# Stage 2 of a three-part network on one Trainium2 core: projections, value tiles, output columns and softmax products at other score units

## The chip, the cores and the metric

The kernel runs on one core of a Trainium2 chip. The metric is the time of one execution on the device in microseconds (us). Five engines with instruction streams of their own work side by side: TensorE (PE, matmuls; PEld its weight loads), VectorE (DVE), ScalarE (ACT), GpSimd (POOL) and SyncE (SP), which issues the DMAs of this kernel. Each runs its instructions in the order in which they stand, and waits on semaphores for the others.

## The reference

Three layers follow each other for a batch of 8, sequence 576, width 512: attention with pooled keys and values, a gated MLP, and a mixture of four causal attention heads ("experts") with the two best of four taken by a gate. The change lies in the last layer:

```python
def _moe2_ref(x, w_gate, wq, wk, wv, wo):
    logits = x @ w_gate                      # top 2 of 4: weights w
    for e in range(E):                       # E = 4, head width 64
        q = x @ wq[e]; k = x @ wk[e]; v = x @ wv[e]
        scores = scale * (q @ k.transpose(0, 2, 1))
        scores = np.where(causal, -1e9, scores)
        scores = scores - scores.max(-1, keepdims=True)
        a = np.exp(scores)
        a /= a.sum(-1, keepdims=True) + 1e-9
        ye = a @ v @ wo[e]
        for kk in range(K):                  # K = 2
            mask = topk[:, :, kk] == e
            out += mask[..., None] * w[:, :, kk:kk + 1] * ye
    return out
```

## The kernel before

Stage 1 (class `PhaseA`) computes the first two layers for all 8 batches and leaves each batch's result in DRAM (`x2`), split into a high and a low part, since products of float32 are made here from three products of such parts. Stage 2 (class `PhaseB`) computes the last layer, batch by batch. Its output is transposed: columns of the result stand on partitions.

Stage 2 takes the four experts in two pairs p. Each batch has 2 x 9 **score units** (p, u): a block of 128 query rows of one expert, u = 1 to 4 of the first expert of the pair, 5 to 8 of the second, and u = 0 the last 64 rows of both. For a unit:

- `score` (L1036 to L1065): two or six matmuls into PSUM (L1047 to L1049, L1059 and L1060), mask and row minimum on VectorE (L1052, L1054, L1061), the exponential on ScalarE (L1064);
- `scale` (L1067 to L1081): the sum's reciprocal on VectorE (L1073, L1075, L1076), then the **softmax product** with that and the gate's weight (L1080), on VectorE for the units that the sets `SDF` (first batch) and `SDL` (last batch) name, on GpSimd for all others;
- `trans` (L1082 on), three units later (`LAG`): transposes on TensorE (L1093, L1106), copied out in a high part by ScalarE and a low part by VectorE (L1097, L1102, L1110, L1111);
- `av`, after the fifth and the last unit of a pair: the products with the values (L1126), two groups of columns.

Between the units stand the other steps, each as a word in a table. `10` to `13` are this batch's projections of pair 1 and `00` to `03` the next batch's of pair 0: q in two halves of the sequence, then k in two halves, twelve matmuls each (L931 to L933), copied out by ScalarE and VectorE. The last k half is followed by four DMAs that put k into the tile `kd` (L971), the last q half by two (L957). `v0` to `v4` are the next batch's **value tiles**, twelve matmuls (L1001 to L1003): three for each of the four chunks kc of its input x, in the order of kc; the gate's logits come with them, and `g` is the gate. `o0` to `o3` are the previous batch's **output columns**, four groups of three matmuls and more (L1148 to L1150), copied out by ScalarE, then stored. `x0` to `x3` load the next batch's four input chunks (L857, 576 KB each) into five slots that are used in turn, and GpSimd copies the last 64 columns of each into a tile for `v4` (L858). With five slots, `x0` finds one that is long free; `x1`, `x2` and `x3` take those that this batch's chunks 0, 1 and 2 leave, whose last reader is `13`.

The table `FILL` has for each p and u the words that follow the unit's scores and the scaling of the unit before; `FIRSTF` is for the first batch, `LASTF` for the last, and `PRE` has the steps ahead of the first unit. `run` goes through the units and writes the steps in this order; a scheduler then sets each engine's order from it, by its own estimates of when data come. It can hold a step's matmuls apart. PSUM has eight banks, each step takes the next that is free. SP's DMAs stand in one queue in the scheduler's order.

Of the kernel before, what the change touches and what calls it, by code (L numbers as in the profile page):

```python
# [822 lines left out]
LAG = 3  # L823
ALV = 1
KDM = 1
FILL = (('', '12 10 11', 'x0', '13 x1 x2 x3', '', '', 'o3 o1 o0', '', ''), ('v0', 'v1 00 02', '01 o2', '03', '', '', '', 'v2 v3', 'v4 g'))
FIRSTF = (('x0 10', '11', '12', '13 x1 x2 x3', '', '', '', '', ''), ('v0 00', '', '01 02 v1', '03', '', '', '', 'v2 v3', 'v4 g'))
LASTF = (('', '10 12 11', '', '', '13', '', 'o1', '', 'o0'), ('', '', '', '', '', 'o2', '', '', 'o3'))
SDF = {(0, 0), (0, 1), (0, 5), (0, 8), (1, 0), (1, 2), (1, 7)}
SDL = {(0, 4), (0, 6), (1, 6), (1, 7)}  # L830
PRE = 'v0 00 01 02 03 v1 v2 v3 v4 g'
AVS = [(0, 256), (256, S)]
LETTER = {mybir.EngineType.PE: "P", mybir.EngineType.Activation: "A", mybir.EngineType.DVE: "V", mybir.EngineType.Pool: "G",
          mybir.EngineType.SP: "S"}
# [5 lines left out]
class PhaseB:  # L840
# [226 lines left out]
    def scale(self, b, p, u):  # L1067
# [6 lines left out]
        else:  # L1074
# [3 lines left out]
        n = min(S, 128 * i + 128)  # L1078
        (nc.vector if (p, u) in (SDF if b == 0 else SDL if b + 1 == B else ()) else
         nc.gpsimd).tensor_scalar(pt[:, :n], pt[:, :n], st[:, 3:4], g, op0=OP.mult, op1=OP.mult)  # L1080
# [86 lines left out]
    def run(self):  # L1167
# [7 lines left out]
        def item(b, x):  # L1175
            if x[0] == "x":
                return [lambda: self.load_x(b + 1, int(x[1]))] if b + 1 < B else []
            if x[0] == "h":
                return [lambda: self.outp_head(int(x[1]))]
            if x[0] == "o":  # L1180
                return [lambda: self.outp(b - 1, int(x[1]))] if b > 0 else []
            if x == "1x":
                return [lambda: self.proj(b, "k", 1, 1, [lambda i=i: self.load_x(b + 1, i) for i in range(4 if b + 1 < B else 0)])]
            if x[0] == "1":
                return [part(b, 1)[int(x[1])]]
            if b + 1 == B:
                return []
            if x[0] == "0":
                return [part(b + 1, 0)[int(x[1])]]
            if x[0] == "v":  # L1190
                return [vpart(b + 1)[int(x[1])]]
            return [lambda: self.gate(b + 1)]
        for x in PRE.split():
            for f in item(0 if x[0] == "1" else -1, x):
                self.step("F", "p" + x, f)
        for k in range(len(units) + LAG + 1):
# [4 lines left out]
            if k < len(units):  # L1201
                b, p, u = units[k]
                for x in (LASTF if b + 1 == B else FILL if b else FIRSTF)[p][u].split():
                    for f in item(b, x):
# [76 lines left out]
```

## Time and profile before

| | us |
|---|---|
| median of 3 runs | 930.12 (929.57 to 930.19) |
| the profiled execution | 929.96 |
| its span, first to last instruction | 928.2 |
| TensorE busy in the span | 912.1 (98%) |
| VectorE busy | 674.5 (73%) |
| ScalarE busy | 515.4 (56%) |
| GpSimd busy | 407.2 (44%) |

The span is what the trace covers; the execution's own time is 1.76 us longer. Stage 2's first matmul starts at 555.24, after that each middle batch takes about 44.8 us. A matmul's busy time overlaps that of the next, so what one adds to TensorE is the distance from its start to the next start, and a wait shows as a start that comes late. The granted clock is 1.00 in all of stage 2 but the last microseconds.

### The profile page before, as it was taken

How to read it: one execution, taken by the hardware profiler on the slowest of the kernel's cores; microseconds unless marked ns; L12 is line 12 of the kernel's file. 1: busy time of each engine (PE TensorE's matmuls, PEld its weight loads, DVE VectorE, ACT ScalarE, POOL GpSimd, SP SyncE). 2: the span in 40 equal slices, each digit the busy share in tenths (PEclk: the TensorE clock that was granted, in tenths of full speed). 3: DMA queues.
4: the chain of work that ended last, by engine and by line, in shares of the span. 5: the costliest groups of instructions: out<-in, count | busy, mean ns of one | idle time of the engine just before them, and what ended most of it. 6: DMA issues, size and time to landing. Idle time of an engine off the chain costs nothing.

```text
span 928.2 us, 18390 instructions
## 1 busy us (share of the span) xinstructions
PE 912.1 (98%) x6518; PEld 858.2 (92%) x6518; DVE 674.5 (73%) x1851; ACT 515.4 (56%) x1273; POOL 407.2 (44%) x604
## 2 busy tenths in 40 slices
PE   8999999999999999999999999999999999999997
PEld 8579899899899899999998999899999999999987
DVE  7989587576676686675775436897878787878785
ACT  5775342443433434334433535677878677777786
POOL 1241576584693693693774440132323232323221
PEclk9999999999999999999999999999999999999999
DMA  9813323124124024033015124434434352514122
GB/s 324 297 57 121 130 74 124 65 85 150 39 74 164 25 74 177 12 111 140 22 43 204 32 90 134 127 115 114 126 104 141 88 154 76 177 52 152 52 63 78
DMA packets 42428, 101.81 MB, mean 110 GB/s; under 512 B 5472, under 2 KB 11616, under 8 KB 41440
## 3 DMA queue, kind: packets, MB, share of 16 engines
q1 hardware_dynamic: 42192, 100.63, 33.6%
q8 instruction: 52, 0.85, 0.4%
q14 instruction: 40, 0.33, 0.1%
q10 hardware_dynamic: 144, 0.00, 0.0%
HBM read 58.67 MB, written 28.31 MB: 94 GB/s over the span
## 4 chain that ended last, share of the span: by engine, by line
PE 80%; DVE 10%; ACT 4%; DMA 3%; issue 2%; SPq 1%; POOL 0%; ACTq 0%; DVEq 0%
PE op L643 4%; PE sc L362 4%; PE sp L615 4%; PE sp L617 4%; PE sp L616 4%; PE op L644 4%; PE op L645 4%; PE av L1126 3%; PE up L599 3%; PE up L601 3%; PE up L600 3%; PE vp L530 3%; PE vp L528 3%; PE vp L529 3%; PE t L1106 2%; PE tr L423 2%
## 5 line engine op out<-in xcount | busy, mean ns | idle before, releaser
L1080 POOL TENSOR_SCALAR pr<-pr,sm,gw 128x128 f32<-128x128 f32 (+3 forms) x119 | 72.1, 608 | 193.5 <-DVE sm L1076 129.8
L1064 ACT ACTIVATE pr<-s,sm 128x256 f32<-128x256 f32 (+4 forms) x160 | 83.1, 521 | 45.6 <-DVE sm L1061 20.7
L615 PE MATMUL sp<-wsh,vnh 128*128 128x288 f32 x256 | 78.0, 305 | 0.0
L643 PE MATMUL op<-g,woh 128*128 128x288 f32 x256 | 76.7, 305 | 0.3 <-DVE x2l L650 0.3
L644 PE MATMUL op<-g,woh 128*128 128x288 f32 x256 | 76.0, 297 | 0.0
L617 PE MATMUL sp<-wsl,vnh 128*128 128x288 f32 x256 | 75.5, 295 | 0.0
L616 PE MATMUL sp<-wsh,vnl 128*128 128x288 f32 x256 | 75.4, 295 | 0.0
L645 PE MATMUL op<-g,wol 128*128 128x288 f32 x256 | 74.3, 295 | 0.0
L599 PE MATMUL up<-x,wih 128*128 128x288 f32 x224 | 67.2, 300 | 0.0
L601 PE MATMUL up<-x,wil 128*128 128x288 f32 x224 | 66.2, 295 | 0.0
L600 PE MATMUL up<-x,wih 128*128 128x288 f32 x224 | 65.7, 293 | 0.0
L1061 DVE CUSTOM_DVE_ANT_0 s<-s,mk 128x512 f32<-128x512 f32 (+3 forms) x128 | 62.3, 487 | 3.0 <-PE t L1106 2.5
L1111 DVE TENSOR_TENSOR pbl<-t,pbh 128x512 fp32r<-128x512 f32 (+3 forms) x128 | 60.4, 484 | 2.3 <-ACT pbh L1110 1.0
L933 PE MATMUL pj<-xb,wql 128*128 128x288 f32 x208 | 61.4, 295 | 0.0
L931 PE MATMUL pj<-xb,wqh 128*128 128x288 f32 x208 | 61.3, 295 | 0.0
L932 PE MATMUL pj<-xb,wqh 128*128 128x288 f32 x208 | 61.2, 294 | 0.0
L1126 PE MATMUL av<-pbh,vt 128*128 128x320 f32 (+4 forms) x224 | 56.0, 279 | 2.7 <-ACT pbh L1110 2.7
L1106 PE MATMUL t<-ident,pr 128*128 128x128 f32 x320 | 56.2, 277 | 2.1 <-POOL pr L1080 2.1
L424 ACT ACTIVATE pth<-tr 128x640 fp32r<-128x640 f32 (+3 forms) x40 | 26.0, 652 | 52.0 <-PE tr L423 42.2
L580 ACT ACTIVATE vnh<-vg,rs 128x512 fp32r<-128x512 f32 (+1 forms) x40 | 27.2, 717 | 47.0 <-POOL rs L562 36.7
L1110 ACT ACTIVATE pbh<-t 128x512 fp32r<-128x512 f32 (+3 forms) x128 | 51.7, 441 | 2.4 <-PE t L1106 1.6
L558 DVE BATCH_NORM_STATS2 bs<-vg 128x6 f32<-128x512 f32 (+1 forms) x40 | 25.9, 681 | 35.6 <-ACT vg L531 35.1
(286 smaller groups left out, 3322.0 us busy)
## 6 DMA issues: line engine op xcount, KB each, us to landing
xb<-x SPq DMA_DIRECT2D x26, 576.0 KB, 5.3
kraw<-k_in SPq DMA_DIRECT2D x16, 576.0 KB, 3.9
x<-x2h SPq DMA_DIRECT2D x32, 288.0 KB, 2.1
x<-x2l SPq DMA_DIRECT2D x32, 288.0 KB, 2.1
kd<-scr SPq DMA_DIRECT2D x64, 144.0 KB, 2.5
out<-o SPq DMA_DIRECT2D x32, 288.0 KB, 2.8
vraw<-v_in SPq DMA_DIRECT2D x16, 512.0 KB, 4.3
pq<-q_in SPq DMA_DIRECT2D x7, 1152.0 KB, 6.9
```

The source lines that it names most:

```text
L599: nc.tensor.matmul(o, self.wi[0][:, kc, c], xh, start=kc == 0, stop=False)
L600: nc.tensor.matmul(o, self.wi[0][:, kc, c], xl, start=False, stop=False)
L601: self.upmm = nc.tensor.matmul(o, self.wi[1][:, kc, c], xh, start=False, stop=kc == 3).ins
L615: nc.tensor.matmul(o, vh[:, k, c], self.ws[0][:, k, s], start=k == 0, stop=False)
L616: nc.tensor.matmul(o, vl[:, k, c], self.ws[0][:, k, s], start=False, stop=False)
L617: nc.tensor.matmul(o, vh[:, k, c], self.ws[1][:, k, s], start=False, stop=False)
L643: nc.tensor.matmul(o, self.wo[0][:, k, c], gh[:, s], start=k == 0, stop=False)
L644: nc.tensor.matmul(o, self.wo[0][:, k, c], gl[:, s], start=False, stop=False)
L645: self.opmm = nc.tensor.matmul(o, self.wo[1][:, k, c], gh[:, s], start=False, stop=k == 3).ins
L1064: nc.scalar.activation(pt[:, s], o, AF.Exp, bias=st[:, 0:1], scale=-1.0, accum_out=st[:, 1 + 4 * j:2 + 4 * j])
L1106: nc.tensor.transpose(ps[:, j], pt[:, 128 * j:128 * j + 128], self.ident)
L1126: nc.tensor.matmul(ps[:, s - lo:], vt[:, j, 2 * p + e].rearrange("p a d -> p (a d)"), t[:, e, j * PTS + s:j * PTS + up], start=j == 0 and ...
```

## The change

The tables say other places. No instruction is added or taken away; five softmax products of the first batch leave VectorE and three come, three of the last batch come.

```diff
-FILL = (('', '12 10 11', 'x0', '13 x1 x2 x3', '', '', 'o3 o1 o0', '', ''), ('v0', 'v1 00 02', '01 o2', '03', '', '', '', 'v2 v3', 'v4 g'))
-FIRSTF = (('x0 10', '11', '12', '13 x1 x2 x3', '', '', '', '', ''), ('v0 00', '', '01 02 v1', '03', '', '', '', 'v2 v3', 'v4 g'))
-LASTF = (('', '10 12 11', '', '', '13', '', 'o1', '', 'o0'), ('', '', '', '', '', 'o2', '', '', 'o3'))
-SDF = {(0, 0), (0, 1), (0, 5), (0, 8), (1, 0), (1, 2), (1, 7)}
-SDL = {(0, 4), (0, 6), (1, 6), (1, 7)}
-PRE = 'v0 00 01 02 03 v1 v2 v3 v4 g'
+FILL = (('x0', '12 10 11', '', '13 x1 x2 x3', '', 'v0', 'o1 o0', 'o3 v1', ''), ('o2 00', '', '01', '02 03', '', '', 'v2', 'v3', 'v4 g'))
+FIRSTF = (('10', '11', 'x0 12', '13 x1 x2 x3', '', '', '', '', ''), ('00 01', 'v0', 'v1', '02 03', '', '', '', 'v2 v3', 'v4 g'))
+LASTF = (('', '10 12 11', '', '', '13', 'o1', '', '', ''), ('', '', '', 'o0', '', 'o2', '', '', 'o3'))
+SDF = {(0, 1), (0, 7), (0, 8), (1, 3), (0, 6)}
+SDL = {(0, 7), (1, 7), (0, 4), (1, 0), (1, 6), (1, 1), (0, 6)}
+PRE = '02 03 v0 v1 00 v2 01 v3 v4 g'
```

What the scheduler makes of it shows best at three places. In the rows below, names are tiles with their numbers: `s` and `s4` scores, `t` transposes, `vp` a value tile, `op` an output column, `xb` and `x4` the input chunks.

TensorE in batch 3, before: the scores of unit (0,5), the transposes of (0,2), the scores of (0,6), and the first matmuls of output column 3:

```order
L1059 MATMUL s_8234<-kd_5859,qs0_5803 128x512
L1060 MATMUL s_8234<-qs0_5803,qzvlo0_5812 128x512
L1106 MATMUL t_8242<-ident_90,pr_5819 128x128 x3
L1059 MATMUL s_8249<-kd_5859,qs0_5803 128x384
L1060 MATMUL s_8249<-qs0_5803,qzvlo0_5812 128x384
L1148 MATMUL op_8258<-ah_7847,wqh_5783 128x256
```

The same place now:

```order
L1059 MATMUL s_8234<-kd_5859,qs0_5803 128x512
L1060 MATMUL s_8234<-qs0_5803,qzvlo0_5812 128x512
L1001 MATMUL vp_8242<-wqh_5783,xb_5782 128x260
L1002 MATMUL vp_8242<-wqh_5783,xb_5782 128x260
L1003 MATMUL vp_8242<-wql_5784,xb_5782 128x260
L1001 MATMUL vp_8242<-wqh_5783,xb_5782 128x260
L1002 MATMUL vp_8242<-wqh_5783,xb_5782 128x260
L1003 MATMUL vp_8242<-wql_5784,xb_5782 128x260
L1106 MATMUL t_8258<-ident_90,pr_5819 128x128 x3
L1059 MATMUL s_8265<-kd_5859,qs0_5803 128x384
L1060 MATMUL s_8265<-qs0_5803,qzvlo0_5812 128x384
L1148 MATMUL op_8274<-ah_7847,wqh_5783 128x256
```

The six matmuls of chunks 0 and 1 of value tile 0 have come in ahead of the transposes, and the first column is column 1.

TensorE in batch 3, before: where chunks 1 to 3 of value tile 0 stood, behind the scores of unit (1,0):

```order
L1001 MATMUL vp_8361<-wqh_5783,xb_5782 128x260
L1002 MATMUL vp_8361<-wqh_5783,xb_5782 128x260
L1003 MATMUL vp_8361<-wql_5784,xb_5782 128x260
L1001 MATMUL vp_8361<-wqh_5783,xb_5782 128x260
L1002 MATMUL vp_8361<-wqh_5783,xb_5782 128x260
L1003 MATMUL vp_8361<-wql_5784,xb_5782 128x260
L1001 MATMUL vp_8361<-wqh_5783,x4_5861 128x260
L1002 MATMUL vp_8361<-wqh_5783,x4_5861 128x260
L1003 MATMUL vp_8361<-wql_5784,x4_5861 128x260
```

Where chunk 2 stands now, within the second output column (column 0), ahead of its last three matmuls:

```order
L1148 MATMUL op_8300<-ah_7847,wqh_5783 128x320
L1149 MATMUL op_8300<-ah_7847,wql_5784 128x320
L1150 MATMUL op_8300<-al_7848,wqh_5783 128x320
L1001 MATMUL vp_8242<-wqh_5783,xb_5782 128x260
L1002 MATMUL vp_8242<-wqh_5783,xb_5782 128x260
L1003 MATMUL vp_8242<-wql_5784,xb_5782 128x260
L1148 MATMUL op_8300<-ah_8186,wqh_5783 128x320
L1149 MATMUL op_8300<-ah_8186,wql_5784 128x320
L1150 MATMUL op_8300<-al_8187,wqh_5783 128x320
```

The value tile is taken apart: chunk 2 in column 0, and chunk 3 in the same way within column 3, behind the scores of unit (0,7).

VectorE in batch 0, before, behind the gate's last copies (`wl`): a reciprocal's sum, a projection's copy (L965), the softmax product of unit (0,0), the scores of (0,3), the product of (0,1):

```order
L1032 COPY wl_6033<-gw_6031 64x2 x2
L1075 TENSOR_SCALAR sm_6068<-sm_6068 128x1
L965 TENSOR_TENSOR qs1_5807<-pj_6109,scr_5820 128x288
L1080 TENSOR_SCALAR pr_5819<-pr_5819,sm_6036,wl_6033 128x576
L1076 RECIPROCAL sm_6068<-sm_6068 128x1
L1061 ISA s_6125,sm_6124<-s_6125,mk_5785 128x256
L1061 ISA sm_6124 128x1
L1080 TENSOR_SCALAR pr_5819<-pr_5819,sm_6068,gw_6031 128x512
L1075 TENSOR_SCALAR sm_6100<-sm_6100 128x1
L965 TENSOR_TENSOR qs1_5807<-pj_6133,scr_5820 128x288
```

The same place now:

```order
L1032 COPY wl_6033<-gw_6031 64x2 x2
L1075 TENSOR_SCALAR sm_6066<-sm_6066 128x1
L965 TENSOR_TENSOR qs1_5807<-pj_6109,scr_5820 128x288
L1076 RECIPROCAL sm_6066<-sm_6066 128x1
L1061 ISA s_6125,sm_6124<-s_6125,mk_5785 128x256
L1061 ISA sm_6124 128x1
L1080 TENSOR_SCALAR pr_5819<-pr_5819,sm_6066,gw_6031 128x512
L1075 TENSOR_SCALAR sm_6098<-sm_6098 128x1
L1076 RECIPROCAL sm_6098<-sm_6098 128x1
L1075 TENSOR_SCALAR sm_6124<-sm_6124 128x1
L1076 RECIPROCAL sm_6124<-sm_6124 128x1
L965 TENSOR_TENSOR qs1_5807<-pj_6133,scr_5820 128x288
```

The product of unit (0,0) is gone (it stands on GpSimd), and the reciprocals of units (0,2) and (0,3) have come ahead of the second projection's copy.

## Rows read from the trace of the kernel before

**Rows 1.** TensorE's waits, 554 to 929: us in total, times, longest.

```profile
PE av L1126 <- ACT pbh L1110: 2.7, 4, 0.9
PE t L1106 <- POOL pr L1080: 2.1, 4, 0.9
PE t L1093 <- DVE sm L1076: 1.5, 1, 1.5
...
PE av L1126 <- DVE pbl L1111: 0.8, 3, 0.4
```

**Rows 2.** Busy time by stretch: length, PE, PEld, DVE, ACT, POOL, clock, DMA.

```profile
568.00:584.00 16.00, 13.17 (x96) 12.07 (x95) 14.57 (x63) 10.88 (x35) 2.88 (x6) 1.00 0.61 172
...
880.00:916.00 36.00, 32.29 (x239) 30.41 (x237) 32.61 (x133) 29.95 (x94) 8.97 (x14) 1.00 0.19 58
```

**Rows 3.** TensorE's timeline, batches 3 and 6: start, us, line, tiles.

```profile
711.51 0.49 PE L1106 MATMUL t<-ident,pr 128*128 128x128 f32 x3
...
714.93 0.31 PE L1148 MATMUL op<-ah,wqh 128*128 128x320 f32 x1
...
853.82 0.28 PE L1001 MATMUL vp<-wqh,x 128*128 128x260 f32 x1
...
854.41 0.28 PE L1003 MATMUL vp<-wql,xb 128*128 128x260 f32 x1
854.76 0.39 PE L1001 MATMUL vp<-wqh,xb 128*128 128x260 f32 x1
```

**Rows 4.** The same view: transposes of unit (0,2) in batches 1, 2, 4, 5, 6.

```profile
621.87 0.49 PE L1106 MATMUL t<-ident,pr 128*128 128x128 f32 x3
...
666.71 0.49 PE L1106 MATMUL t<-ident,pr 128*128 128x128 f32 x3
...
756.36 0.49 PE L1106 MATMUL t<-ident,pr 128*128 128x128 f32 x3
...
801.21 0.49 PE L1106 MATMUL t<-ident,pr 128*128 128x128 f32 x3
...
846.03 0.49 PE L1106 MATMUL t<-ident,pr 128*128 128x128 f32 x3
```

**Rows 5.** SP's timeline: issues of chunk 2 (batches 2 to 6) and kd's copies.

```profile
666.66 0.53 SPq L857 DMA_DIRECT2D x<-x  x1
...
708.91 2.52 SPq L971 DMA_DIRECT2D kd<-scr  x4
711.54 0.52 SPq L857 DMA_DIRECT2D xb<-x  x1
...
756.37 1.03 SPq L857 DMA_DIRECT2D xb<-x  x2
...
801.52 1.02 SPq L857 DMA_DIRECT2D xb<-x  x2
...
846.17 1.01 SPq L857 DMA_DIRECT2D xb<-x  x2
```

**Rows 6.** Those five loads, us to landing (last column); then all of line 857.

```profile
x<-x SPq DMA_DIRECT2D x1, 576.0 KB, 5.4
...
xb<-x SPq DMA_DIRECT2D x1, 576.0 KB, 6.3
...
xb<-x SPq DMA_DIRECT2D x1, 576.0 KB, 5.6
...
xb<-x SPq DMA_DIRECT2D x1, 576.0 KB, 4.4
...
xb<-x SPq DMA_DIRECT2D x1, 576.0 KB, 7.2
...
DMA to landing us min/median/max: 4.0/5.3/7.9
```

**Rows 7.** GpSimd's timeline, batches 0 and 1: in brackets the idle time before.

```profile
582.47 0.45 POOL L1080 TENSOR_SCALAR pr<-pr,sm,gw 128x128 f32<-128x128 f32 x1 [0.15 <-ACT pr L1064]
...
623.03 0.29 POOL L858 CAST xb<-xb 128x128 fp32r<-128x128 f32 x1 [1.91 <-DMA xb<-x]
```

**Rows 8.** VectorE's timeline, batch 0: the product of unit (0,0).

```profile
577.49 0.57 DVE L1080 TENSOR_SCALAR pr<-pr,sm,wl 128x576 f32<-128x576 f32 x1
```

## The prediction

> **What bounds.** I read the busy time by stretch first, then TensorE's waits, then its timeline at the places that the change moves, and last the load queue. Batches of stage 2 are counted 0 to 7; "unit (p, u)" is score unit u of head pair p. In the first stretch of stage 2, 568 to 584, TensorE (PE) is busy 13.17 of 16 us, in the last batch, 880 to 916, 32.29 of 36 [rows 2]; all its waits from 554 on, by releaser, are the few of [rows 1]: 3.5 us for the attention-value products and 3.6 us for transposes that want a softmax product are what matters, the longest 1.5 us. So stage 2 is bound by TensorE, whose instructions the change leaves the same in number and shape: it can gain only what is left of such waits, and it can lose wherever a matmul is put ahead of its data. The reader should therefore ask of each moved step one thing: when does the datum land, and when does TensorE now come to ask for it?
>
> **Value tile 0 in the middle batches.** This is the large term. The value tile for the next batch (L1001 to L1003, twelve matmuls, three for each chunk kc of its input x) stood behind unit (1,0); now its first two chunks stand behind unit (0,5), right ahead of the transposes of unit (0,2), its third inside output column 0 and its fourth inside column 3, as the order in the section on the change shows. Before, TensorE reached the second chunk in batch 6 at 853.82, which is 7.8 us after those transposes at 846.03 [rows 3, 4].
>
> When does it now ask for chunk 2, the third? In batch 3 the transposes begin at 711.51, and the tenth matmul of the second output column begins 3.42 us later, at 714.93 [rows 3]; between these lie just the matmuls that now stand ahead of chunk 2 (transposes, score, one whole column, nine matmuls of the next). Ahead of them stand six value matmuls at 0.12 us: the five starts from 853.82 to 854.41 are 0.59 us [rows 3]. So chunk 2 is asked for 4.14 us after the start of the transposes as it was before.
>
> When does it land? Chunk 2 can't be loaded before the k projection of pair 1 has let go of its slot, and on SP's queue its issue stands behind four copies into kd that wait for that projection's copy-out: in batch 3 the copies are issued from 708.91 on, the load at 711.54 [rows 5]. The change leaves this piece of SP's queue as it was. The load then takes 4.4 to 7.2 us [rows 6]. Asked for against landed, batch by batch (starts from [rows 3, 4], issues from [rows 5], time to landing from [rows 6]):
> - batch 2: 666.71 + 4.14 = 670.85 against 666.66 + 5.4 = 672.06: waits 1.21
> - batch 3: 715.65 against 711.54 + 6.3 = 717.84: 2.19
> - batch 4: 760.50 against 756.37 + 5.6 = 761.97: 1.47
> - batch 5: 805.35 against 801.52 + 4.4 = 805.92: 0.57
> - batch 6: 850.17 against 846.17 + 7.2 = 853.37: 3.20
>
> Together 8.64 us. In batch 1 nine matmuls come ahead of the transposes of 621.87 [rows 4], so chunk 2 is asked for 0.72 us later, at 622.59; GpSimd's copy of that chunk, which sat waiting for the load, began at 623.03 [rows 7]: 0.44. Sum +9.1 us. That TensorE stops on such a load, and for how long, one place of the kernel before shows: in batch 6 the last chunk's first matmul starts at 854.76, 0.35 us after the one before it instead of 0.12 [rows 3]. That wait goes (0.23, and about 0.1 on the next matmul), since the chunk is now asked for later than chunk 2's end: −0.3. Chunk 3 lands behind chunk 2 and is asked for about 1.7 us later in TensorE's order; I cost it at nothing, and if it lands later than that the rest is added. Bounds of the load: from 4.0, the least of all x loads [rows 6], which leaves next to nothing, to 7.9, the longest there, some 2.1 us a batch more than the mean of the five. I take the five as they were, since what is queued ahead is the same. A wait of TensorE here can't be filled by anything: the engines run in order. It gives VectorE and ScalarE time, but they bind nowhere near.
>
> [...]
>
> **Other moves in the middle.** Columns 1, 0, 3, 2 stand one to three units later or in other order, value tiles 1 to 3 earlier, q and k projections a unit later. The number of TensorE's matmuls between a score and its transposes stays or grows nearly everywhere, and no wait of [rows 1] rests on them. Zero, with ±1 for what I can't see.
>
> **First batch.** The products of units (0,0), (0,5), (1,0), (1,2), (1,7) leave VectorE for GpSimd; (0,6), (0,7), (1,3) come the other way. The product of unit (0,0) took VectorE 0.57 us at 577.49, and the first transposes waited for that engine 1.5 us [rows 8, 1]. On GpSimd it takes longer but stands alone there. The waits that follow end with the product of unit (0,4), which began on GpSimd at 582.47 [rows 7], behind a reciprocal that VectorE gets to after four copies out of PSUM. VectorE now has 0.5 us less ahead of that reciprocal, but four small reciprocal steps for units (0,2) and (0,3) stand ahead of it too (some 0.3), so this chain ends only 0.2 earlier: waits merge, they don't go. Later in the batch five products have left VectorE and three have come, on balance some 1 us less of its work, and the projections are spread; I take another −0.7 off the attention-value waits of [rows 1]. Together −0.9, between −2.5 and +0.5.
>
> **Last batch.** Output column 1 now stands ahead of the transposes of unit (0,2), column 0 behind the scores of unit (1,3): both leave the run between, units (0,6) to (1,3), where their matmuls gave VectorE time, and VectorE takes on three products, (0,7), (1,0), (1,1), at 0.4 to 0.57 us. VectorE is busy 32.61 of 36 us there [rows 2]. On the other side, column 0 now covers a wait of 0.9 us, the longest for ScalarE's copy ahead of the value products [rows 1]. 1.5 of VectorE's work less about 0.8 of cover: +0.7, between −1 and +2.5.
>
> **Sum.** The profiled execution took 929.96 us, 0.16 under the median of 930.12. 929.96 + 9.1 − 0.3 − 0.9 + 0.7 = 938.6.
>
> **Rivals.**
> - The loads land early (not slower). Price: with 4.0 us to landing [rows 6] chunk 2 is there before it is asked for in batches 2, 3, 4 and 6, and 0.17 late in batch 5; with batch 1's 0.44 the term is 0.6, and the time 929.96 + 0.6 − 0.3 − 0.9 + 0.7 = 930.1. It decides at 4.1 us from issue. For it: the quickest x load took 4.0; against: the five that are queued behind kd's copies took 4.4 or more. [...] 0.10.
> - The first batch is freed (faster). As above, and GpSimd has the products of units (0,2) to (0,4) done by the time TensorE comes to them, so that the transposes' waits, up to 3.6 us, go: 929.96 + 0.6 − 0.3 − 3.6 = 926.7. It decides at VectorE's reciprocal for unit (0,4), before 582.1. Against: that engine is busy 14.57 of 16 us there [rows 2]. 0.08.
> - The last batch is bound by VectorE too. If the 3.1 us of columns that left the run aren't cover any more and the three products all show, some 4 us come instead of 0.7: 942 to 943. For it: 32.61 of 36. 0.12.
> - My forecast, loads as they were: 0.70, by itself 934.5 to 942.
>
> **Numbers.** About 0.2% is what a measurement of this kernel tells from no change. Slower by more: 0.70 + 0.12 = 0.82; within: 0.10; faster: 0.08. The range leaves out the first two rivals: 933.5 to 943.5.
>
> **What would show it.** In the profile after: a TensorE wait on x's load at L1001 in each of batches 2 to 6, 0.5 to 3.2 us long, put down to the DMA, in the midst of an output column; TensorE's waits for a DMA sum to about 9 us; the batches' period grows by about 1.8 us. If those matmuls start without a gap, the forecast is wrong, and the time lies near 930. The first batch's wait ahead of the first transposes stays over 1 us; the last batch shows new waits between units (0,6) and (1,3) and none, or a short one, at the value products of pair 0.

## The result, and the profile after

The changed kernel takes 937.0 us, the median of six runs from 934.5 to 939.6, beside 929.74 for the kernel before in the same comparison: a ratio of 1.0077, 95% interval 1.0067 to 1.0088, 7.3 us more. The forecast was 938.6, the range 933.5 to 943.5. The profiled execution took 936.62 us, 6.66 more than that of the kernel before.

TensorE's waits in stage 2 of the changed kernel, 554 to 936 us (who waits for whom: us in total, times, longest):

```profile
PE vp L1001 <- DMA xb<-x: 6.7, 4, 2.3
PE t L1106 <- POOL pr L1080: 3.1, 4, 1.7
PE av L1126 <- ACT pbh L1110: 1.4, 2, 0.8
PE t L1093 <- POOL pr L1080: 1.2, 1, 1.2
PE av L1126 <- DVE pbl L1111: 0.9, 4, 0.4
...
PE vp L1001 <- DMA x<-x: 0.4, 1, 0.4
```

The first and the last line are new against [rows 1]: five waits of a value tile for a load, 7.1 us in all. They stand in TensorE's timeline at these five matmuls, one in each of batches 2 to 6; in brackets the idle time before and what ended it:

```profile
670.28 0.39 PE L1001 MATMUL vp<-wqh,x 128*128 128x260 f32 x1 [0.40 <-DMA x<-x]
...
717.25 0.39 PE L1001 MATMUL vp<-wqh,xb 128*128 128x260 f32 x1 [1.78 <-DMA xb<-x]
...
764.86 0.39 PE L1001 MATMUL vp<-wqh,xb 128*128 128x260 f32 x1 [2.29 <-DMA xb<-x]
...
811.20 0.39 PE L1001 MATMUL vp<-wqh,xb 128*128 128x260 f32 x1 [1.12 <-DMA xb<-x]
...
857.91 0.39 PE L1001 MATMUL vp<-wqh,xb 128*128 128x260 f32 x1 [1.50 <-DMA xb<-x]
```

Each is the first matmul of chunk 2 of value tile 0, within output column 0, where the prediction had put it. The idle time leaves out some 0.15 us that a start comes later by than after a matmul without a wait; counted from the start before less the usual distance the five are late by 0.56, 1.94, 2.45, 1.28 and 1.67, together 7.9 us. This "late start" is the measure used below, since the prediction's asking times are starts too. The loads that they wait for, in the same order (last column: us from issue to landing), and the 19 loads of line 857 issued from 655 to 860 us:

```profile
x<-x SPq DMA_DIRECT2D x1, 576.0 KB, 4.7
...
xb<-x SPq DMA_DIRECT2D x1, 576.0 KB, 6.0
...
xb<-x SPq DMA_DIRECT2D x1, 576.0 KB, 6.4
...
xb<-x SPq DMA_DIRECT2D x1, 576.0 KB, 4.5
...
xb<-x SPq DMA_DIRECT2D x1, 576.0 KB, 5.8
...
  PE vp L1001: 7.1, 5
...
DMA to landing us min/median/max: 4.1/5.0/7.3
```

As in [rows 6] the same load in the same place lands after anything from 4.5 to 6.4 us.

At the start of stage 2 TensorE's timeline shows the two waits that stand in place of those of the first batch in [rows 1]:

```profile
578.02 0.76 PE L1093 MATMUL t<-ident,pr 128*128 128x128 f32 x5 [1.15 <-POOL pr L1080]
...
582.73 0.33 PE L1106 MATMUL t<-ident,pr 128*128 128x128 f32 x1 [1.69 <-POOL pr L1080]
```

The first transposes now wait 1.15 us for GpSimd instead of 1.5 for VectorE, and the wait that follows has grown to 1.69. Together they are as long as the four before them (1.50, 0.26, 0.92 and 0.16 us); the last one ends at 582.73 instead of 582.97, of which 0.04 us is stage 2's earlier start (555.20 instead of 555.24).

### The profile page after: what moved, and what is told of

The parts are those of the page before. It is cut to its first block, busy times and chain, and to the rows that moved or that the text cites. A ratio compares the mean times of both kernels' runs of the same rounds, so it can differ in the third digit from the quotient of the medians.

```text
span 934.8 us, 18384 instructions
## 1 busy us (share of the span) xinstructions
PE 912.3 (98%) x6518; PEld 857.3 (92%) x6518; DVE 672.4 (72%) x1852; ACT 518.6 (55%) x1273; POOL 408.8 (44%) x603
## 4 chain that ended last, share of the span: by engine, by line
PE 86%; DMA 5%; DVE 4%; ACT 3%; issue 1%; SPq 0%; POOL 0%; POOLq 0%; ACTq 0%; DVEq 0%
PE sc L362 4%; PE av L1126 4%; PE op L643 4%; DMA xb<-x 4%; PE sp L615 4%; PE sp L617 4%; PE sp L616 4%; PE op L644 4%; PE op L645 4%; PE up L599 3%; PE up L601 3%; PE up L600 3%; PE t L1106 3%; PE pj L931 3%; PE pj L933 3%; PE pj L932 3%
## 5 line engine op out<-in xcount | busy, mean ns | idle before, releaser
L1080 POOL TENSOR_SCALAR pr<-pr,sm,gw 128x128 f32<-128x128 f32 (+2 forms) x117 | 71.5, 613 | 194.3 <-DVE sm L1076 113.6
L1064 ACT ACTIVATE pr<-s,sm 128x256 f32<-128x256 f32 (+4 forms) x160 | 83.2, 521 | 40.3 <-DVE sm L1075 18.2
```

## Experiments

### The three parts, each alone

Theory A: the time is lost on chunk 2 of value tile 0, asked for before it lands. Rivals: it is lost in the first and last batches (B), or by the other moves in the middle ones (C). The first run takes the table of the middle batches alone into the kernel before:

```diff
-FILL = (('', '12 10 11', 'x0', '13 x1 x2 x3', '', '', 'o3 o1 o0', '', ''), ('v0', 'v1 00 02', '01 o2', '03', '', '', '', 'v2 v3', 'v4 g'))
+FILL = (('x0', '12 10 11', '', '13 x1 x2 x3', '', 'v0', 'o1 o0', 'o3 v1', ''), ('o2 00', '', '01', '02 03', '', '', 'v2', 'v3', 'v4 g'))
```

> The kernel before with the middle batches' table alone. Theory A (the loss is TensorE waiting for chunk 2 of value tile 0): TensorE's waits for a DMA at L1001 in batches 2 to 6 sum to 6 to 10 us, as the 7.9 us of late starts in the changed kernel, and the time is 929.7 + 7.5 = 937.2 (935 to 940). Rival B (the loss is in the first and last batches' tables and the softmax products): within 1 us of 929.7.

Measured 937.11 us against 929.64, ratio 1.0083 (1.0069 to 1.0096): the whole loss. In its profiled execution, its quickest with 935.97, the late starts at L1001 for a load sum to 5.3 us, under the 6 to 10 expected. B falls.

The second goes the other way: the changed kernel, with value tiles 0 and 1 back where they were.

```diff
-... '', 'v0', 'o1 o0', 'o3 v1', ''), ('o2 00', '', '01', ...
+... '', '', 'o1 o0', 'o3', ''), ('v0 o2 00', 'v1', '01', ...
```

> The changed kernel with value tiles 0 and 1 of the middle batches back behind units (1,0) and (1,1), all else as changed. Theory A: the DMA waits go, 7.9 us of them, so 937.0 - 7.9 = 929.1 (928 to 930.5), and the runs lie close together again. Rival C (the moves of columns and projections cost as well): the DMA waits go but 932 or more remains.

Measured 928.08 us, ratio 0.9983 (0.9974 to 0.9992), all eleven runs between 927.85 and 928.50. C falls as the cause of the loss: columns and projections stand where the change put them, and the loss is gone, with every wait for a load. (Value tile 1 went back as well; the run with the loads ahead, further down, keeps it where the change put it, and the loss is gone there too.) TensorE's waits of this run from 554 us on, complete:

```profile
PE t L1106 <- POOL pr L1080: 3.1, 4, 1.7
PE av L1126 <- ACT pbh L1110: 1.4, 2, 0.8
PE t L1093 <- POOL pr L1080: 1.1, 1, 1.1
PE av L1126 <- DVE pbl L1111: 1.1, 5, 0.4
PE pj L931 <- issue: 0.9, 1, 0.9
```

The first and the last batch, each alone in the kernel before:

```diff
-FIRSTF = (('x0 10', ...   SDF = {(0, 0), (0, 1), (0, 5), ...   PRE = 'v0 00 01 02 03 ...
+FIRSTF = (('10', '11', 'x0 12', ...   SDF = {(0, 1), (0, 7), ...   PRE = '02 03 v0 v1 00 ...
```

> The kernel before with the first batch's tables alone (steps, softmax products, order ahead of the first unit). The prediction put -0.9 on it; by the late starts of TensorE up to 620 us in the two traces it should be -1.3: 928.4 (927.9 to 929.2). Rival: these moves cost, 930.5 or more.

Measured 928.34 us, ratio 0.9988 (0.9979 to 0.9996): −1.30. The waits of the first transposes hardly shrink, 2.8 us in the view before and after. By late starts, most of the gain stands at three places of the kernel before: the value products at 597.57 and 618.11 us, with what follows each, give back 0.33 and 0.37 us, and a value tile's first matmul at 602.14, with the next, 0.45.

```diff
-LASTF = (('', '10 12 11', '', '', '13', '', 'o1', '', 'o0'), ('', '', '', '', '', 'o2', '', '', 'o3'))
-SDL = {(0, 4), (0, 6), (1, 6), (1, 7)}
+LASTF = (('', '10 12 11', '', '', '13', 'o1', '', '', ''), ('', '', '', 'o0', '', 'o2', '', '', 'o3'))
+SDL = {(0, 7), (1, 7), (0, 4), (1, 0), (1, 6), (1, 1), (0, 6)}
```

> The kernel before with the last batch's tables alone (columns and softmax products). The prediction put +0.7 on it: 930.4. By the late starts after 872 us in the two traces, 5.82 before and 5.85 after, nothing: 929.7 +- 0.4. Rival (the last batch is bound by VectorE): 932 or more.

Measured 928.70 us, ratio 0.9988 (0.9979 to 0.9997): −0.94. Both expectations missed, the prediction's cost of 0.7 and the zero read from the two traces; what stands behind it comes further down.

### Is it landing less asking?

If theory A holds in its numbers, a later asking shortens the waits by as much. In this run value tile 0 stands two units later than the change put it:

```diff
-... 'v0', 'o1 o0', 'o3 v1', ''), ...
+... '', 'o1 o0', 'v0 o3 v1', ''), ...
```

> The changed kernel with value tile 0 two units later, behind unit (0,7). By the order and the changed kernel's landings chunk 2 is asked for 1.0 us later than there, chunk 3 only 0.85 us behind chunk 2, while it lands 1.3 to 1.5 us behind it. Theory A: waits for chunk 2 of 0, 0.8, 1.3, 0.1 and 0.5 us, and up to 0.6 a batch for chunk 3, together some 5 us: 937.0 - 2.9 = 934.1 (932 to 936). Rival (only chunk 2 is ever late): 937.0 - 4.5 = 932.5 or less.

Measured 934.46 us (931.56 to 938.03), ratio 1.0061 (1.0047 to 1.0075), within the range of theory A and above the rival's 932.5. The interval overlaps the changed kernel's, so the time alone doesn't show a gain. The profiled execution, the quickest of the six, shows what the rival left out. TensorE's timeline in batch 4, chunks 2 and 3:

```profile
762.21 0.39 PE L1001 MATMUL vp<-wqh,xb 128*128 128x260 f32 x1 [0.56 <-DMA xb<-x]
...
763.62 0.39 PE L1001 MATMUL vp<-wqh,xb 128*128 128x260 f32 x1 [0.31 <-DMA xb<-x]
```

Chunk 2 has become a shorter wait, in part because it is asked for later and in part because its load took 5.4 us here instead of 6.4; behind it chunk 3 is late too, since the two are now asked for closer together than they land. Of the waits for a load in this execution, five with 1.7 us, four are chunk 3's.

### Why does it land late?

Two runs in which TensorE's instructions stand in the same order throughout. For that value tile 0 was written as three steps, `va` (chunks 0 and 1), `vb` (chunk 2) and `vc` (chunk 3), so that the scheduler can't move its chunks. The first is the partner:

```diff
-... 'v0', 'o1 o0', 'o3 v1', ''), ...
+... 'va', 'o1 o0 vb', 'o3 vc v1', ''), ...
```

> The changed kernel with value tile 0 written as three steps at fixed places: chunks 0 and 1 as changed, chunk 2 right behind column 0, chunk 3 behind column 3. It is the partner of the next run. Chunk 2 is asked for three matmuls (0.44 us) later than in the changed kernel; its DMA waits of 0.40, 1.78, 2.29, 1.12 and 1.50 us become 0, 1.3, 1.9, 0.7 and 1.1, some 5 us in all. Theory A (a wait is the landing minus the asking): 937.0 - 2.2 = 934.8 (933 to 936.5). Rival (the wait has to do with where the matmul stands, in the midst of a column): 930 or less.

Measured 933.81 us (931.05 to 935.91), ratio 1.0043 (1.0029 to 1.0057), 1 us under the expectation. Though chunk 2 stands behind a whole column now, the waits remain, so the rival falls (L1001 is line 1003 of this kernel):

```profile
PE vp L1003 <- DMA xb<-x: 4.1, 3, 2.2
...
PE vp L1003 <- DMA x<-x: 1.0, 1, 1.0
```

Such a wait can cost more than its own length. In batch 3 of this run TensorE waited for 2.22 us, and 1.2 us after it went on, its granted clock fell from 1.00 (2.4 GHz) to 0.50 (1.2 GHz), from 719.6 to 723.0 us. First the wait, then two matmuls in that stretch and two after it, then a row of the busy time by stretch, whose 0.50 is the clock:

```profile
718.42 0.39 PE L1003 MATMUL vp<-wqh,xb 128*128 128x260 f32 x1 [2.22 <-DMA xb<-x]
...
722.22 0.42 PE L1004 MATMUL vp<-wqh,x 128*128 128x260 f32 x1
722.44 0.42 PE L1005 MATMUL vp<-wql,x 128*128 128x260 f32 x1
...
723.53 0.28 PE L1003 MATMUL vp<-wqh,xb 128*128 128x260 f32 x1
723.65 0.28 PE L1004 MATMUL vp<-wqh,xb 128*128 128x260 f32 x1
```

```profile
719.60:722.90 3.30, 3.30 (x17) 3.30 (x16) 1.09 (x5) 1.38 (x6) 0.84 (x2) 0.50 0.48 184
```

The starts lie 0.22 us apart instead of 0.12; over the 17 matmuls of the stretch that is some 1.5 us. In the profile of the changed kernel the clock stayed at 1.00 in spite of a wait of 2.29 us, so the 7.9 us there hold none of this, and what decides whether the clock falls is not shown.

The second run changes the order of SP's queue: the loads of chunks 1 to 3 are issued between the matmuls of `13` and the copies into kd. GpSimd's copies from these chunks (L858) move with them; TensorE, VectorE and ScalarE keep their order.

```diff
-... '13 x1 x2 x3', '', 'va', 'o1 o0 vb', 'o3 vc v1', ''), ...
+... '1x', '', 'va', 'o1 o0 vb', 'o3 vc v1', ''), ...
-... self.load_x(b + 1, i) for i in range(4 if b + 1 < B else 0)])]
+... self.load_x(b + 1, i) for i in range(1, 4 if b + 1 < B else 0)])]
```

> As the run before, with TensorE's order the same, but SP issues the loads of chunks 1 to 3 ahead of the four copies into kd, some 4.3 us earlier. Theory A (chunk 2 is late since its issue stands behind those copies): it lands before it is asked for, the waits at L1001 go, and the time is 928 to 930. Rival (the DMA engines' rate sets the landing; three loads side by side take that much longer): waits of 3 to 5 us remain, 933 to 935.

Measured 928.37 us (927.95 to 928.62), ratio 0.9984 (0.9976 to 0.9993): 5.4 us less than its partner, by the order of one queue. SP's timeline in batch 3, first of the changed kernel, then of this run:

```profile
706.81 0.53 SPq L857 DMA_DIRECT2D xb<-x  x1
708.58 2.55 SPq L971 DMA_DIRECT2D kd<-scr  x4
711.24 0.52 SPq L857 DMA_DIRECT2D xb<-x  x1
```

```profile
705.86 1.03 SPq L857 DMA_DIRECT2D xb<-x  x2
707.00 0.37 SPq L857 DMA_DIRECT2D x<-x  x1
707.60 2.52 SPq L971 DMA_DIRECT2D kd<-scr  x4
```

Where chunk 2 was issued at 711.24 in the changed kernel, after a wait of 1.2 us for the projection's copy-out (L964) and 2.55 us in which the four copies were issued, here chunks 1 and 2 go out together from 705.86 on, and the copies into kd come behind. (This run is some 0.9 us ahead by then.) Who waited for the loads of batches 2 to 6, and how long they took to land:

```profile
who waited for it (us, times):
  POOL xb L858: 22.2, 15
...
DMA to landing us min/median/max: 4.3/5.0/8.4
```

TensorE isn't among those that wait any more; GpSimd is, for its copies of the last 64 columns. The median of the loads is 5.0 us as before; chunk 2's five took 5.0 to 5.3 us, 25.7 in all instead of 27.4. So it is the earlier issue, some 3.5 to 4 us a batch, that took the waits away, and the rival falls: three loads side by side do not take that much longer.

### The last batch, taken apart

In the prediction this term was a cover less a cost. One run has only the new places of the columns, one only the new engines of the products:

```diff
-LASTF = (('', '10 12 11', '', '', '13', '', 'o1', '', 'o0'), ('', '', '', '', '', 'o2', '', '', 'o3'))
+LASTF = (('', '10 12 11', '', '', '13', 'o1', '', '', ''), ('', '', '', 'o0', '', 'o2', '', '', 'o3'))
```

> The kernel before with the last batch's output columns alone at their new places; its softmax products stay on the engines they had. The two tables of the last batch together gave 0.94 us, where the prediction had a cost of 0.7. Theory P (the gain is column 0's cover of the 0.9 us wait at the value products of pair 0, L1126): that wait goes here as well, and the time is 928.8 +- 0.4, unless units (0,7), (1,0) and (1,1), still on GpSimd, now come late. Rival Q (the columns that left units (0,6) to (1,3) uncover GpSimd's products): TensorE's waits at L1106 for GpSimd grow past the 1.4 us of the run with both tables, 930.0 or more.

Measured 928.48 us against 930.00, ratio 0.9983 (0.9974 to 0.9992): −1.5.

```diff
-SDL = {(0, 4), (0, 6), (1, 6), (1, 7)}
+SDL = {(0, 7), (1, 7), (0, 4), (1, 0), (1, 6), (1, 1), (0, 6)}
```

> The kernel before with the last batch's softmax products alone on their new engines: three more on VectorE, the columns as before. The prediction priced these three at 1.5 us of VectorE's work in a stretch in which it is busy 32.6 of 36 us. If that shows: 930.5 to 931.2. Rival (they lie under the columns, or take a wait for GpSimd away): 929.7 +- 0.3, or less.

Measured 930.51 us, ratio 1.0007 (0.9998 to 1.0015): some 0.5 more, not clear of nothing. Its profiled execution took 932.33 us, more than any other of its runs; the granted clock fell to 0.50 for 3.4 us in its first 20, long before the last batch. TensorE's waits from 872 us on, first of the kernel before, then with the columns alone, then with columns and products:

```profile
PE av L1126 <- ACT pbh L1110: 2.4, 3, 0.9
PE t L1106 <- POOL pr L1080: 0.7, 1, 0.7
PE av L1126 <- DVE pbl L1111: 0.7, 2, 0.4
```

```profile
PE av L1126 <- ACT pbh L1110: 1.4, 2, 0.8
PE t L1106 <- POOL pr L1080: 0.5, 1, 0.5
PE av L1126 <- DVE pbl L1111: 0.3, 1, 0.3
```

```profile
PE av L1126 <- ACT pbh L1110: 1.4, 2, 0.8
PE t L1106 <- POOL pr L1080: 1.4, 3, 0.5
PE av L1126 <- DVE pbl L1111: 0.3, 1, 0.3
```

3.8 us, 2.2 and 3.1. The columns take away the 0.9 us wait at the value products of pair 0 and 0.6 besides; the products bring 0.9 us back, as waits for products that are still on GpSimd. The time agrees: from the scores of unit (1,7) of batch 6 (L1060, at 872.28 in the kernel before) to the last matmul it takes 52.08 us before, 50.47 with the columns alone and 51.11 with both, and 52.74 with the products alone: 1.6 less for the columns, 0.65 more for the products, either way. Theory P holds, Q falls. How the products cost time is seen at the product of unit (0,8) in GpSimd's timeline, with the columns alone and with both:

```profile
899.62 0.45 POOL L1080 TENSOR_SCALAR pr<-pr,sm,gw 128x128 f32<-128x128 f32 x1 [0.72 <-ACT pbh L1110]
```

```profile
899.92 0.45 POOL L1080 TENSOR_SCALAR pr<-pr,sm,gw 128x128 f32<-128x128 f32 x1 [4.45 <-DVE sm L1076]
```

It begins 0.3 us later, on VectorE's reciprocal (L1076), ahead of which the product of unit (0,7), 0.41 us long, now stands on VectorE; GpSimd itself has been idle for 4.45 us by then. TensorE's transposes of that product start at 900.43 instead of 900.12. At transposes further on, 908.98 instead of 908.34, it is 0.64; the product that these wait for came behind ScalarE's exponential (L1064), and where this second half comes from was not followed further.

### Do the parts add up, and the best of them

The changed ends without the changed middle:

```diff
+FIRSTF, LASTF, SDF, SDL and PRE as changed; FILL as before
```

> The kernel before with the changed tables of the first and the last batch, and its own for the middle ones. If the two gains of 1.30 and 0.94 us measured apart add up, 929.64 - 2.24 = 927.4 (927.0 to 927.8), the fastest of all. Rival (the middle table is needed for the last batch's gain): 928.3 or more.

Measured 927.63 us (927.35 to 927.90) against 929.72, ratio 0.9976 (0.9968 to 0.9985). That is the fastest of all here, and 2.09 of the 2.24 us expected. With the columns alone in the last batch it might be quicker still; that was not run.

With the middle table's 7.5 the sum of the parts is 929.7 + 7.5 − 1.3 − 0.9 = 935.0, and 937.0 had been measured. So the changed kernel and the one with its middle table alone ran once more, side by side, without an edit:

> The changed kernel once more, beside the next run on one chip: its middle table alone cost 7.5 us, the ends gave 1.3 and 0.9, which makes 934.9, but 937.0 was measured. If the 2 us between is the spread of the loads' landing: 933.5 to 937.5 here, some 2 us under the next run. If the parts hinder each other: 937 again, like the next run.

> The kernel before with the middle batches' table alone, once more: 937.1 was measured, from 936.0 to 938.0. Spread of the landing: between 935 and 938.5, some 2 us above the changed kernel in this comparison; otherwise like it.

Measured 935.68 us (935.22 to 937.30) and 936.28 (936.02 to 938.44), beside 930.00. The gap of 2 us to the sum is mostly gone for the changed kernel, and the table alone came out a little lower as well; their difference, 0.6 us, is less than the 2 us expected of it, but with five runs each and a spread of over 2 us this doesn't decide. The versions that wait for the loads range over 2 to 6.5 us from run to run, the two that were freed of that wait (928.08 and 928.37 us) over 0.65 and 0.67. Part of that spread is the clock and not the landing: of the changed kernel's first six runs the two slowest (937.98 and 939.63 us) had a mean granted clock of 0.997 and 0.998, the other four, at 1.00, range over 2.9 us.

## Why the prediction was right, point by point

**What bounds.** TensorE, whose waits alone can change the time: so it was. Against the run with the value tiles put back, whose ends are the same, the profiled execution is 8.3 us longer (936.62 and 928.31); the late starts of 7.9 us and some 0.1 us on the matmul behind each of them (717.25 to 717.47 in batch 3, instead of 0.12) make 8.4.

**Value tile 0.** The mechanism, the place and the batches were right, and the size nearly: 9.1 forecast, 7.9 us in the profiled execution. By its two factors:

| batch | asked for after issue, forecast | measured | landing, before | after | wait, forecast | measured |
|---|---|---|---|---|---|---|
| 2 | 4.19 | 4.22 | 5.4 | 4.7 | 1.21 | 0.56 |
| 3 | 4.11 | 4.07 | 6.3 | 6.0 | 2.19 | 1.94 |
| 4 | 4.13 | 4.03 | 5.6 | 6.4 | 1.47 | 2.45 |
| 5 | 3.83 | 3.28 | 4.4 | 4.5 | 0.57 | 1.28 |
| 6 | 4.00 | 4.15 | 7.2 | 5.8 | 3.20 | 1.67 |

(Asked for: the start in the timeline less the late start, against the issue in SP's timeline.) Landing less asking gives 0.48, 1.93, 2.37, 1.22 and 1.65: each measured wait to within 0.1 us. The asking time, read by counting what stands between two starts, held to 0.15 us but for batch 5, where SP issued one of the copies into kd for 1.57 us and the load went out late. The landing did not repeat batch by batch, and could not have been forecast from one trace; only its sum did, 28.9 us against 27.4. Batch 1, forecast at 0.44, had no such wait in this execution, and one of 0.69 in the second profile of the changed kernel. Over the table alone, the term was 8.8 with the wait of batch 6 taken off, and 7.5 and 6.3 us were measured: somewhat large. That wait of batch 6, priced at −0.3, was read from one execution: the five other profiles with the old middle table have no such late start there. That the copies ahead of it on SP's queue are the reason, the two runs with the same order on TensorE show. I took that piece of the queue as given and asked no further; its order alone gives the whole term back.

**Other moves in the middle.** Nil, ±1: the version with the value tiles put back takes 928.08, the one with the whole middle table as before 927.63. Their intervals overlap and they were not run side by side, so a cost is not shown; but the runs of the two hardly overlap (927.85 to 928.50 and 927.35 to 927.90), and a cost of some 0.5 us may well be there.

**First batch.** −0.9 forecast, −1.3 measured (interval −2.0 to −0.4). That the early waits merge rather than go was right in the trace: counted from stage 2's start, the last of them ends 0.2 us earlier, as forecast. The −0.7 came about, 0.33 and 0.37 by late starts, but it could not be read from [rows 1]: of its 3.5 us of attention-value waits only 0.3 stand before 620 us. That size was luck. The 0.45 at the value tile I had not seen.

**Last batch.** Here a step failed: +0.7 was forecast, −0.94 measured, just within its bound of −1. Both terms were mis-sized, the cover at 0.8 where the columns alone gave 1.5, the three products at 1.5 where they cost some 0.5. I priced the products at VectorE's whole time for them, because that engine was busy 32.6 of 36 us [rows 2]. Where the trace shows how a product costs time, it is by way of the reciprocal that it delays: 0.3 us at unit (0,8), where the product is 0.41 long. A busy share says that such a delay is likely, not how much of it is waited for. The rival that has the last batch bound by VectorE, at 942 to 943, falls. The sign named for this batch came in the main: two new waits for softmax products, 0.53 and 0.43 us at 903.56 and 908.46 of the changed kernel, and the 0.9 us wait at the value products of pair 0 is gone (an earlier one of 0.64 there stays).

**The rivals.** "The loads land early" would have needed 4.1 us to landing; the five took 4.5 to 6.4. "The first batch is freed" falls with it, and the transposes' wait of 1.69 us stayed.

**The sum.** 9.1 − 0.3 − 0.9 + 0.7 = 8.6 forecast; the parts alone gave 7.5 − 1.3 − 0.9 = 5.3, and the changed kernel as a whole 7.3 and, the second time, 5.7. So the three terms together were put 3.3 us too high, by 1.6 in the last batch, 1.3 in the middle and 0.4 in the first; that the first measurement of the whole lay only 1.6 us under the forecast is luck with the spread from run to run; the second lay 2.9 under it.

## What to carry to other kernels

When an order moves a matmul ahead, compare two times for its operand: when the engine will come to ask, which could be counted from the starts in the trace to 0.15 us in four of five batches, and when the load lands, which has to be taken as a range, since it varies from run to run. Look also at what stands ahead of the load in its queue: here copies that waited and then took their time to be issued, 1.2 and 2.55 us in batch 3; changing the order of that queue was worth as much as moving the consumer. And a wait of TensorE can cost more than its length, as where the granted clock fell behind one. Price work that goes to a busy engine by what stands behind it there and who waits for that, not by the busy share.

## What the runs showed of the hardware

A load of 576 KB took from 4.0 to 7.9 us to land in the kernel before [rows 6] and from 4.1 to 7.3 in the changed one, with copies and another load beside it. Where TensorE waits for it, that passes to the time of the whole kernel, whose runs in the first comparison spread over 5.1 us instead of 0.6, or over 2.9 without the two at a granted clock under 1.00.

The copies into kd took longer where they stood behind three loads. First the changed kernel, then the run with the loads ahead, the 36 copies of line 971 from 655 to 860 us, of which the 20 of pair 1 are those that moved:

```profile
DMA to landing us min/median/max: 2.2/3.0/4.3
```

```profile
DMA to landing us min/median/max: 2.2/6.6/7.9
```

A median of 6.6 us instead of 3.0 (for the four of pair 1 in batch 3 alone, 7.1 instead of 3.2), and TensorE waited for none of them: the scores of pair 1 that read kd come far enough behind.

TensorE's granted clock fell to 0.50 for 3.4 us in the middle of stage 2 in one profile, 1.2 us after a wait of 2.22 us, and not in another with a wait of 2.29; matmuls of 260 columns then started 0.22 us apart instead of 0.12.
